# Another order for the first layer's step: low part of g on VectorE, gathered decode, Tanh first

## The chip, the cores and the metric

One core of one Trainium2 chip runs the whole program. The metric is the device time of one execution in microseconds (us); the kernel before took 1130.29 us in the median of 3 runs (1128.52 to 1130.34).

## The reference

Three stages, each feeding the next, on 1792 tokens of width 768 (4 batches of 448, 12 heads of 64):

```python
scores = (q @ k.T) / sqrt(64) - log(448)
x = (1 / (1 + exp(-scores))) @ v           # sigmoid attention, no softmax
h = x @ w_in                               # first layer, 768 -> 2048
x = (h - tanh(h)) @ w_out                  # 2048 -> 768
gate = 1 / (1 + exp(-(x @ w_gate)))        # second layer, 768 -> 1536
out = (gate * (x @ w_val)) @ w_out2        # 1536 -> 768
```

The weights arrive as 64-bit words that the kernel turns into float32 itself. Where h is small, h - tanh(h) cancels, so the kernel replaces it there by a polynomial in h.

## The kernel before, in words

Every operand of a product is held as two parts: a rounded high part and a low part, the value minus its high part. A product is three matmuls (high x high, high x low, low x high; `mm3`, L363 to 368, whose matmuls all have L365).

The attention stage runs first. The first layer then runs as 32 steps, i = 0 to 31: the hidden features are cut into 8 pairs of 128-blocks, and each pair is run for the 4 batches in turn (i // 4 is the pair, i % 4 the batch). In iteration i of the loop (L899 to L939) TensorE computes the hidden product of step i+1 (`hidden_mm`, tile ph, 36 matmuls) and then the output product of step i in six groups of six matmuls, one per block of 128 output columns (`project_group`, tiles po, index 0 to 5). Beside it, ScalarE, VectorE and GpSimd turn ph of step i+1 into g, which is the operand of the next iteration's output product.

The order on each engine is written out by hand: it is the order in which the program issues the instructions, and each engine runs its own in that order. What the functions issue:

- `hidden_act` (L385) gives ScalarE's `sq` (u = Square of ph, L399), `th` (y = Tanh, L402), `cut` (mask mk from u, L405), `q1` and `q2` (two inner squares s from the mask, L408, L411), and VectorE's `a` (y = h - Tanh, L414), `b` (L417, needs u), `c` (L422, needs the first inner square), `d` (L427, needs the second) and `e`: the mask copy COPY_PREDICATED (L432, writes y where the mask holds), after which ScalarE makes the high part of g (L433). `f` is the low part of g (L437), two GpSimd instructions of half the columns; it is issued one iteration later, as `rest` (L907).
- `step` (L502) places all of this among the six groups. Groups 1, 3 and 5 are evicted into the accumulator by ScalarE (`post`, L523), and before that their bank is filled with the old accumulator by ScalarE (a seed: `seed`, L454, `pre` in `step`); groups 0, 2 and 4 are evicted with an add by VectorE (L472). Seeds exist in steps 4 to 28; from step 29 on all groups are evicted by VectorE. The po tiles share four PSUM banks, and a new tile takes the bank that the program let go first.
- `decode1` (L182) turns one first-layer weight into its two parts, one weight per iteration: Abs on ScalarE (L145), four VectorE instructions (L148, L151, L157, L163), the fetch of a later weight by SP (L135), and then the split: a copy on ScalarE (L175) and two low parts on GpSimd (L178). There is one tile m for all of them. The pieces stand at fixed places: Abs in `ex[2]`, the VectorE pieces at the head of the next iteration (`todo`), the split in `ex[0]`.
- `keeping` (L196) decodes a weight of the second layer ahead of time in four pieces: Abs on ScalarE; the two mask steps (L148, L151); the first merge (L157); the second merge (L163) with the next fetch and the store to DRAM on SP (kept, L215). There is one tile mk for it, so the next Abs must wait for the store. `some` (L895) issues these pieces, two at the head of an iteration, the third in `ex[1]`, the fourth in `ex[2]`; three iterations of four do one weight (and all from 24 to 26).
- From iteration 27 on (`tail`) the places `ex` also hold work for the second layer: the load and split of its first weights, the operands (L592, L594) and sums (L578).

Of the kernel before, what the change touches and what calls it, by code (L numbers as in the profile page):

```python
# [8 lines left out]
F32 = mybir.dt.float32  # L9
# [3 lines left out]
ALU = mybir.AluOpType  # L13
# [19 lines left out]
def kernel(  # L33
# [12 lines left out]
    nc = tc.nc  # L46
# [135 lines left out]
    def decode1(u):  # L182
        m = dp.tile([128, WC], I32, tag="m", name=f"m{u}", padded_shape=[128, 2 * WC])

        def d():
            n, w = w_alloc(f"w{u}", [128, 2, KD, 128])
            rounded(w, m.bitcast(F32), f"w{u}")
            w_t[u] = n, w

        a, b, c, c2 = decode(u, m)  # L190
        return [a, b, lambda: (c(), c2()), d]

    kept = {}
    early = []
# [175 lines left out]
    def hidden_mm(i):  # L370
        g, t = divmod(i, NB)
        ph = psa.tile([128, 2, 512], F32, tag="pa", name=f"ph{i}")
        for j in range(2):
            n, w = w_t[4 * g + j]
            for c in range(KD):
                xt = x[t][c // KH]
                mm3(
                    ph[:, j, :S], lambda a: w[:, a, c], lambda a: xt[:, a, c % KH],
                    c == 0, c == KD - 1,
                )  # L380
            if t == NB - 1:
                w_free.append(n)
        h_t[i] = ph

    def hidden_act(i):  # L385
        ph = h_t.pop(i)
        h = ph[:, :, :S]
        gt = gp.tile([128, 2, 2, S], F32R, tag="g", name=f"g{i}")
        if i == 0:
            gp.tile([128, GGAP], F32, tag="ggap", name="ggap", bufs=1)  # L390
        g_t[i] = gt
        uu = tp.tile([128, 2, S], F32, tag="u", name=f"u{i}")
        y = tp.tile([128, 2, S], F32, tag="y", name=f"y{i}")
        mk = tp.tile([128, 2, S], F32, tag="mk", name=f"mk{i}")
        s1 = tp.tile([128, 2, S], F32, tag="s1", name=f"s1{i}")
        s2 = tp.tile([128, 2, S], F32, tag="s2", name=f"s2{i}")

        def sq():
            nc.scalar.activation(out=uu, in_=h, func=AF.Square)  # L399

        def th():
            nc.scalar.activation(out=y, in_=h, func=AF.Tanh)  # L402

        def cut():
            nc.scalar.activation(out=mk, in_=uu, func=AF.Relu, bias=gb[:, 2:3], scale=-1.0)  # L405

        def q1():
            nc.scalar.activation(out=s1, in_=mk, func=AF.Square, bias=gb[:, 0:1], scale=-1.0)  # L408

        def q2():  # L410
            nc.scalar.activation(out=s2, in_=mk, func=AF.Square, bias=gb[:, 1:2], scale=-1.0)  # L411

        def a():
            nc.vector.tensor_tensor(out=y, in0=h, in1=y, op=ALU.subtract)  # L414

        def b():
            nc.vector.scalar_tensor_tensor(  # L417
                out=h, in0=uu, scalar=G_C, in1=h, op0=ALU.mult, op1=ALU.mult
            )

        def c():
            nc.vector.scalar_tensor_tensor(  # L422
                out=h, in0=s1, scalar=G_B1, in1=h, op0=ALU.add, op1=ALU.mult
            )

        def d():
            nc.vector.scalar_tensor_tensor(  # L427
                out=h, in0=s2, scalar=G_B2, in1=h, op0=ALU.add, op1=ALU.mult
            )

        def e():
            nc.vector.copy_predicated(y, mk.bitcast(I32), h)  # L432
            nc.scalar.activation(out=gt[:, 0], in_=y, func=AF.Copy)  # L433

        def f():
            for j in range(2):
                nc.gpsimd.tensor_tensor(  # L437
                    out=gt[:, 1, j], in0=y[:, j], in1=gt[:, 0, j].bitcast(F32), op=ALU.subtract
                )

        return [sq, th, cut, q1, q2], [a, b, c, d, e, f]

# [9 lines left out]
    def seed(name, at, d):  # L452
        po = pb_tile(name)
        nc.scalar.activation(out=po[:, :S], in_=at[:, d], func=AF.Copy)  # L454
        return po

    def project_group(name, at, gt, outs, d, first, dst=None, po=None, evict=True):

        seeded = po is not None
        if not seeded:  # L460
            po = pb_tile(name)
        for j, (_, w) in enumerate(outs):
            mm3(
                po[:, :S], lambda a: w[:, a, d], lambda a: gt[:, a, j],
                j == 0 and not seeded, j == len(outs) - 1, seeded,
            )
        if not evict:
            return po
        if first:
            nc.vector.tensor_copy(out=at[:, d], in_=po[:, :S])  # L470
        else:
            nc.vector.tensor_tensor(out=at[:, d], in0=po[:, :S], in1=at[:, d], op=ALU.add)  # L472
        if dst is not None:
            nc.sync.dma_start(out=dst, in_=at[:, d])
# [4 lines left out]
    def outs1(i):  # L479
        g, t = divmod(i, NB)  # L480
        if g == 0:
            acc[t] = acc_tile(t, f"acc{i}")
        return acc[t], g_t.pop(i), [w_t[4 * g + 2], w_t[4 * g + 3]]
# [13 lines left out]
    def run(fs):  # L497
        for f in fs:
            f()
        fs.clear()  # L500

    def step(i, act, dve, extra, po):  # L502

        g, t = divmod(i, NB)
        at, gt, outs = outs1(i)
        sq, th, cut, q1, q2 = act
        a, b, c, d_, e = dve

        def pre(d):
            if g and i < LASTSEED:  # L510
                po[d] = seed(f"po{i}_{d}", at, d)

        def group(d):
            by_act = d % 2 == 1 and i < LASTSEED
            p = project_group(
                f"po{i}_{d}", at, gt, outs, d, g == 0, None, po.get(d), not by_act
            )
            po[d] = p

        def post(d):  # L520
            if i >= LASTSEED:
                return
            nc.scalar.activation(out=at[:, d], in_=po[d][:, :S], func=AF.Copy)  # L523

        ex = extra + [None] * 6
        sq()
        th()
        group(0)
        a()
        pre(3)  # L530
        cut()
        group(1)
        b()
        run(ex[0] or [])
        group(2)
        q1()
        post(1)
        c()
        run(ex[1] or [])
        pre(5)  # L540
        q2()
        group(3)
        d_()
        run(ex[2] or [])
        post(3)
        group(4)
        e()
        run(ex[3] or [])
        group(5)
        post(5)  # L550
        run(ex[4] or [])
        if t == NB - 1:
            w_free.extend(n for n, _ in outs)

# [268 lines left out]
    with tc.manual_schedule():  # L823
# [19 lines left out]
        todo = []  # L843
        nxt = [0]
        for p in range(NP):
# [3 lines left out]
            if p >= 3 and not todo and nxt[0] < NEARLY:  # L849
                todo = decode1(nxt[0])  # L850
# [36 lines left out]
        todo = []  # L887
# [4 lines left out]
            early += keeping(j)  # L892
        TAIL = N1 - 5

        def some(kind):  # L895
            if early and len(early) % 4 == kind and (i < TAIL or kind) and (i % 4 or i > TAIL - 4):
                early.pop(0)()

        for i in range(N1 - 1):  # L899
            hidden_mm(i + 1)  # L900
            po = {}
            if NB <= i < LASTSEED:
                po[1] = seed(f"po{i}_1", acc[i % NB], 1)
            if todo:
                todo.pop(0)()
            if rest:
                rest.pop()()  # L907
            if todo:
                todo.pop(0)()
            some(0)  # L910
            some(3)
            act, dve = hidden_act(i + 1)
            ex = [[], [], [], [], []]
            if todo:
                ex[0].append(todo.pop(0))
                nxt[0] += 1
            if nxt[0] < wanted(i + 1):
                todo = decode1(nxt[0])
                ex[2].append(todo.pop(0))
            ex[1].append(lambda: some(2))  # L920
            ex[2].append(lambda: some(1))
            rest = [dve.pop()]
            tail = i - TAIL
            if tail == 0:
                ex[3].append(lambda: load_m(0))
            elif tail == 1:
                for at in range(4):
                    ex[at].append(first_split.pop(0))
            elif tail == 2:
                ex[0].append(lambda: operand(0, "a11", nc.vector))  # L930
                ex[1].append(first_split.pop(0))
                ex[2].append(first_split.pop(0))
            elif tail == 3:
                operand(0, "s1", nc.gpsimd)
                operand(0, "s2", nc.gpsimd)
                ex[2].append(lambda: operand(0, "a12", nc.gpsimd))
                ex[3].append(lambda: sums("s4"))
                ex[4].append(lambda: sums("s3"))
            step(i, act, dve, ex, po)  # L939
        rest.pop()()  # L940
        tp_ctx.close()
# [99 lines left out]
```

## Time and profile before

| what | value |
|---|---|
| median of 3 runs | 1130.29 us (1128.52 to 1130.34) |
| the profiled execution's own time | 1127.33 us |
| its span, first to last instruction | 1125.4 us |
| granted TensorE clock, mean | 0.998 |
| busy TensorE / VectorE / ScalarE / GpSimd | 1091.5 / 806.8 / 608.8 / 522.7 us |

The profile is one execution. A busy share is an average over all stages, so this document reads the first layer's loop (about 153 to 628 us) alone. In the rows, PE is TensorE's matmul, PEld its weight load, DVE VectorE, ACT ScalarE, POOL GpSimd, SP the engine that issues DMAs; "out<-in" gives the tiles, L the line; in brackets stands how long the engine was idle before and whose end released it.

### The profile page before, as it was taken

The numbers are of one execution on the slowest core, as the hardware profiler recorded it, in microseconds if no ns is written. First come the engines' busy times: TensorE is split into PE (matmuls) and PEld (weight loads), VectorE is DVE, ScalarE is ACT, GpSimd is POOL, SyncE is SP. The second block draws the span as 40 slices with busy tenths as digits, with TensorE's granted clock in tenths as the row PEclk, the third lists the DMA queues.
The fourth block names the chain that finished last, engine by engine and source line by source line (L and its number), as shares of the span: only waits on it lengthen the run. The fifth ranks groups of instructions, "written<-read, shape, count | busy, mean of one in ns | idle before, by whom it ended". The sixth has DMA issues, their size and how long they took to land.

```text
span 1125.4 us, 15990 instructions
## 1 busy us (share of the span) xinstructions
PE 1091.5 (97%) x6085; PEld 967.6 (86%) x6085; DVE 806.8 (72%) x1083; ACT 608.8 (54%) x855; POOL 522.7 (46%) x475
## 2 busy tenths in 40 slices
PE   9999989999999999999999989999998999999998
PEld 5677779888989898988898888998997899999997
DVE  4778646888898888889867988988468545354444
ACT  6778645666667676667666444444336234334320
POOL 5455301433433343443336657675466755446540
PEclk9999999999999999999999999999999999999999
DMA  7766301424232324233320156464112411111202
GB/s 197 188 187 190 112 1 43 141 98 129 87 124 90 121 99 140 98 118 121 116 68 29 59 172 218 149 209 163 55 46 69 142 70 56 57 56 62 80 1 98
DMA packets 40204, 119.79 MB, mean 106 GB/s; under 512 B 6080, under 2 KB 21440, under 8 KB 40128
## 3 DMA queue, kind: packets, MB, share of 16 engines
q1 hardware_dynamic: 36896, 116.38, 31.8%
q0 software_dynamic: 3072, 2.17, 0.9%
q8 instruction: 48, 0.79, 0.3%
q10 hardware_dynamic: 160, 0.23, 0.1%
q14 instruction: 28, 0.23, 0.1%
HBM read 99.09 MB, written 19.66 MB: 106 GB/s over the span
## 4 chain that ended last, share of the span: by engine, by line
PE 60%; DVE 14%; ACT 9%; DMA 9%; issue 5%; POOL 3%; SPq 1%; ACTq 0%; DVEq 0%; POOLq 0%
PE pq L365 14%; PE ph L365 10%; DMA kept<-mk 8%; PE pb L365 6%; PE po L365 6%; PE pa L365 6%; PE pc L365 5%; PE pv L349 5%; PE sa L314 4%; PE pe L365 3%; DVE ph L422 2%; DVE ph L427 2%; ACT mk L405 1%; ACT y L402 1%; PE sl L326 1%
## 5 line engine op out<-in xcount | busy, mean ns | idle before, releaser
L365 PE MATMUL po<-g,w 128*128 128x448 f32 x1152 | 247.7, 367 | 10.3 <-DVE acc L472 6.0
L365 PEld LDWEIGHTS po<-g,w 128*128 128x128 f32 x1152 | 211.7, 188 | 40.5 <-POOL g L437 11.6
L365 PE MATMUL ph<-x,w 128*128 128x448 f32 x1152 | 235.8, 362 | 0.2 <-ACT at L318 0.2
L365 PEld LDWEIGHTS ph<-x,w 128*128 128x128 f32 x1152 | 215.8, 187 | 15.3 <-ACT at L318 0.6
L437 POOL TENSOR_TENSOR g<-y,g 128x448 fp32r<-128x448 f32 x64 | 114.0, 1801 | 194.8 <-issue 166.1
L365 PE MATMUL pq<-gg,w 128*128 128x448 f32 x864 | 183.8, 363 | 5.1 <-POOL gg L742 2.4
L365 PEld LDWEIGHTS pq<-gg,w 128*128 128x128 f32 x864 | 161.4, 187 | 18.7 <-POOL gg L742 3.1
L178 POOL TENSOR_TENSOR w_t<-mm,w_t 128x384 fp32r<-128x384 f32 x92 | 101.1, 1128 | 119.7 <-ACT w_t L175 54.1
L178 POOL TENSOR_TENSOR w<-m,w 128x384 fp32r<-128x384 f32 x64 | 63.6, 1017 | 113.2 <-ACT w L175 80.9
L472 DVE TENSOR_TENSOR acco<-pq,acco 128x448 f32<-128x448 f32 x120 | 72.2, 619 | 33.4 <-PE pq L365 32.9
L365 PE MATMUL pa<-a,w_b 128*128 128x448 f32 x432 | 94.2, 362 | 0.0
L365 PEld LDWEIGHTS pa<-a,w_b 128*128 128x128 f32 x432 | 81.0, 187 | 5.4
L472 DVE TENSOR_TENSOR acc<-po,acc 128x448 f32<-128x448 f32 x93 | 57.3, 618 | 26.6 <-PE po L365 26.6
L433 ACT ACTIVATE g<-y 128x896 fp32r<-128x896 f32 x32 | 30.6, 956 | 81.3 <-DVE y L432 81.3
L318 ACT ACTIVATE at<-sa,bias_s 128x896 f32<-128x896 f32 x72 | 67.3, 1008 | 8.0 <-PE sa L314 7.9
L178 POOL TENSOR_TENSOR w<-mm,w 128x384 fp32r<-128x384 f32 x44 | 48.5, 1124 | 45.5 <-ACT w L175 43.3
L742 POOL TENSOR_TENSOR gg<-sg,gg 128x448 fp32r<-128x448 f32 x44 | 62.5, 1451 | 12.3 <-ACT gg L739 12.3
L175 ACT ACTIVATE w_t<-mm 128x768 fp32r<-128x768 f32 x48 | 40.0, 842 | 48.5 <-DVE mm L646 34.8
L175 ACT ACTIVATE w_b<-mm 128x768 fp32r<-128x768 f32 (+1 forms) x48 | 32.5, 680 | 62.2 <-PE pb L365 30.0
L178 POOL TENSOR_TENSOR w_b<-mm,w_b 128x384 fp32r<-128x384 f32 x46 | 51.3, 1138 | 23.1 <-ACT w_b L175 12.1
L349 PE MATMUL pv<-at,vt 128*64 128x224 f32 x576 | 61.0, 362 | 0.0
L349 PEld LDWEIGHTS pv<-at,vt 128*64 128x64 f32 x576 | 39.9, 139 | 19.8 <-issue 8.3
(102 smaller groups left out, 1880.2 us busy)
## 6 DMA issues: line engine op xcount, KB each, us to landing
mm<-kept SPq DMA_DIRECT2D x36, 768.0 KB, 4.2
st<-in_w_out_dram SPq DMA_DIRECT2D x28, 768.0 KB, 4.5
st<-in_w_in_dram SPq DMA_DIRECT2D x16, 768.0 KB, 4.3
st<-in_w_gate_dram SPq DMA_DIRECT2D x12, 768.0 KB, 4.9
st<-in_w_val_dram SPq DMA_DIRECT2D x12, 768.0 KB, 5.0
kept<-mk SPq DMA_DIRECT2D x21, 384.0 KB, 5.6
kept<-mq SPq DMA_DIRECT2D x15, 384.0 KB, 5.5
kt<-in_k_dram SPq DMA_DIRECT2D x48, 112.0 KB, 4.0
```

The costliest lines, as they stand in the source:

```text
L175: nc.scalar.activation(out=w0, in_=mf, func=AF.Copy)
L178: (low or nc.gpsimd).tensor_tensor(out=w1[:, r], in0=mf[:, r], in1=w0[:, r].bitcast(F32), op=ALU.subtract)
L314: nc.tensor.matmul(pa[:, j, :S], kk[r, ki, c], qq[r, qi], start=(i == 0), stop=(i == 2),)
L318: nc.scalar.activation(out=at[:, :, c], in_=pa[:, :, :S], func=AF.Sigmoid, bias=bias_s, scale=qk_scale,)
L349: nc.tensor.matmul(po[j * D:(j + 1) * D, h, :SH], vt[:, j, c], at[:, j, c, h * SH:(h + 1) * SH], start=False, stop=(c == NCH - 2),)
L365: nc.tensor.matmul(o, w(i), xv(j), start=first and n == 0, stop=last and n == 2, skip_group_check=seeded,)
L422: nc.vector.scalar_tensor_tensor(out=h, in0=s1, scalar=G_B1, in1=h, op0=ALU.add, op1=ALU.mult)
L427: nc.vector.scalar_tensor_tensor(out=h, in0=s2, scalar=G_B2, in1=h, op0=ALU.add, op1=ALU.mult)
L433: nc.scalar.activation(out=gt[:, 0], in_=y, func=AF.Copy)
L437: nc.gpsimd.tensor_tensor(out=gt[:, 1, j], in0=y[:, j], in1=gt[:, 0, j].bitcast(F32), op=ALU.subtract)
L472: nc.vector.tensor_tensor(out=at[:, d], in0=po[:, :S], in1=at[:, d], op=ALU.add)
L742: low.tensor_tensor(out=gt[t][:, 1, j], in0=sg[t][:, j], in1=gt[t][:, 0, j].bitcast(F32), op=ALU.subtract,)
```

## The change

The low part of g becomes one VectorE instruction over all 896 columns instead of two GpSimd instructions. In the step, Tanh goes ahead of Square; the mask and then the seed of group 3 follow; `b` and the first inner square come ahead of group 1; the eviction `post(1)` and the second inner square come ahead of group 2; and the split of the decoded weight (`ex[0]` before, `ex[1]` now) stands behind the second inner square and the seed of group 5. `some` goes: the four pieces of a second-layer weight are issued together at the head of the iteration, behind the low part of g and the first-layer decode, which follow the mask copy on VectorE. The number of weights decoded so early stays the same.

```diff
         def f():
-            for j in range(2):
-                nc.gpsimd.tensor_tensor(
-                    out=gt[:, 1, j], in0=y[:, j], in1=gt[:, 0, j].bitcast(F32), op=ALU.subtract
-                )
+            nc.vector.tensor_tensor(
+                out=gt[:, 1], in0=y, in1=gt[:, 0].bitcast(F32), op=ALU.subtract
+            )
...
-        ex = extra + [None] * 6
+        th()
         sq()
-        th()
         group(0)
         a()
+        cut()
         pre(3)
-        cut()
+        b()
+        q1()
         group(1)
-        b()
-        run(ex[0] or [])
-        group(2)
-        q1()
+        run(extra[0])
         post(1)
         c()
-        run(ex[1] or [])
+        q2()
+        group(2)
         pre(5)
-        q2()
+        run(extra[1])
         group(3)
         d_()
-        run(ex[2] or [])
+        run(extra[2])
         post(3)
...
-        def some(kind):
-            if early and len(early) % 4 == kind and (i < TAIL or kind) and (i % 4 or i > TAIL - 4):
-                early.pop(0)()
-
...
-            some(0)
-            some(3)
+            if early and i < TAIL and (i % 4 or i > TAIL - 4):
+                run(early[:4])
+                del early[:4]
             act, dve = hidden_act(i + 1)
             ex = [[], [], [], [], []]
             if todo:
-                ex[0].append(todo.pop(0))
+                ex[1].append(todo.pop(0))
                 nxt[0] += 1
...
-            ex[1].append(lambda: some(2))
-            ex[2].append(lambda: some(1))
             rest = [dve.pop()]
```

## Rows read from the trace of the kernel before

**Rows 1.** Busy us in one decode step: length, PE, PEld, DVE, ACT, POOL, clock, DMA, GB/s

```profile
376.13:391.70 15.57, 15.02 (x74) 13.27 (x73) 13.44 (x17) 10.45 (x16) 5.74 (x4) 1.00 0.41 127
```

**Rows 2.** Timeline of TensorE: start us, length us, engine, line, operation, tiles, count [idle, releaser]

```profile
167.24 7.36 PE L365 MATMUL ph<-x,w 128*128 128x448 f32 x36
...
475.10 7.39 PE L365 MATMUL po<-g,w 128*128 128x448 f32 x36
...
489.52 5.28 PE L365 MATMUL po<-g,w 128*128 128x448 f32 x24
495.25 2.75 PE L365 MATMUL po<-g,w 128*128 128x448 f32 x12 [0.45 <-DVE acc L472]
...
603.71 7.36 PE L365 MATMUL ph<-x,w 128*128 128x448 f32 x36
```

**Rows 3.** Who waited for whom over the whole span: us in total, times, longest

```profile
ACT mk L145 <- DMA kept<-mk: 40.8, 15, 3.9
...
ACT m L145 <- POOL w L178: 3.3, 6, 0.6
```

**Rows 4.** Timeline of all engines in a decode step that lost time

```profile
490.03 0.90 ACT L145 ACTIVATE mk<-st 128x768 f32<-128x768 f32 x1 [2.58 <-DMA kept<-mk]
...
494.58 0.62 DVE L472 TENSOR_TENSOR acc<-po,acc 128x448 f32<-128x448 f32 x1
```

**Rows 5.** Timeline, a VectorE merge beside GpSimd's low part of g

```profile
409.60 3.75 POOL L437 TENSOR_TENSOR g<-y,g 128x448 fp32r<-128x448 f32 x2 [4.58 <-issue]
...
410.53 1.80 DVE L163 SCALAR_TENSOR_TENSOR m<-st,m 128x768 int32<-128x768 int32 x1
```

**Rows 6.** Groups of instructions by shape, whole span: count, busy us, mean ns

```profile
L178 POOL TENSOR_TENSOR w<-m,w 128x384 fp32r<-128x384 f32 x64 | 63.6, 1017 | 113.2 <-ACT w L175 80.9 <-PE po L365 32.2
...
L163 DVE SCALAR_TENSOR_TENSOR mk<-st,mk 128x768 int32<-128x768 int32 x21 | 20.0, 952 | 0.0
...
L178 DVE TENSOR_TENSOR w_t<-mm,w_t 128x768 fp32r<-128x768 f32 x2 | 1.9, 954 | 0.0
```

**Rows 7.** Timeline of ScalarE in an undisturbed step, T = 475.10

```profile
475.30 0.92 ACT L399 ACTIVATE u<-ph 128x896 f32<-128x896 f32 x1 [2.69 <-PE ph L365]
476.11 0.91 ACT L402 ACTIVATE y<-ph 128x896 f32<-128x896 f32 x1
...
476.91 0.56 ACT L454 ACTIVATE po<-acc 128x448 f32<-128x448 f32 x1
...
477.37 1.05 ACT L405 ACTIVATE mk<-u,gb 128x896 f32<-128x896 f32 x1
...
478.31 0.84 ACT L175 ACTIVATE w<-m 128x768 fp32r<-128x768 f32 x1
479.04 1.04 ACT L408 ACTIVATE s<-mk,gb 128x896 f32<-128x896 f32 x1
...
479.98 0.54 ACT L523 ACTIVATE acc<-po 128x448 f32<-128x448 f32 x1
...
480.40 0.55 ACT L454 ACTIVATE po<-acc 128x448 f32<-128x448 f32 x1
```

**Rows 8.** Timeline, two ScalarE neighbours of which the second needs the first

```profile
614.80 1.04 ACT L405 ACTIVATE mk<-u,gb 128x896 f32<-128x896 f32 x1
...
615.87 1.04 ACT L408 ACTIVATE s<-mk,gb 128x896 f32<-128x896 f32 x1
```

**Rows 9.** Timeline of step 28, where the seed of group 5 came late

```profile
581.67 6.17 PE L365 MATMUL po<-g,w 128*128 128x448 f32 x30
...
587.38 0.56 ACT L454 ACTIVATE po<-acc 128x448 f32<-128x448 f32 x1
...
589.31 7.36 PE L365 MATMUL ph<-x,w 128*128 128x448 f32 x36
```

**Rows 10.** The page's DMA issues: count, KB each, us to landing

```profile
kept<-mk SPq DMA_DIRECT2D x21, 384.0 KB, 5.6
```

**Rows 11.** Timeline, TensorE at the tail's first wait for GpSimd

```profile
612.99 6.68 PE L365 MATMUL po<-g,w 128*128 128x448 f32 x32 [1.12 <-POOL g L437]
```

More of the change, by code (lines that the diff above doesn't have):

```diff
@@ L547, in step @@
         e()
-        run(ex[3] or [])
+        run(extra[3])
         group(5)
         post(5)
-        run(ex[4] or [])
+        run(extra[4])
         if t == NB - 1:
```

## The prediction

> **What bounds the kernel now.** I first asked for the busy times by stretch: in a first-layer step of 15.57 us that also decodes a weight for the second layer, TensorE is busy 15.02 us, VectorE 13.44, ScalarE 10.45, GpSimd 5.74, at granted clock 1.00 [rows 1]. TensorE is the bound, so the change can be worth only what a step takes beyond its matmuls. How long these take is in the order of TensorE's work: an undisturbed step (hidden product, then six groups of six matmuls) takes 603.71 - 589.31 = 14.40 us [rows 2, 9]; from the second hidden product (167.24) to the last (603.71) 29 steps take 436.47 us where 29 x 14.40 = 417.6 would do [rows 2]. **18.9 us are lost**, 0.65 a step, and this is all that the loop can give back.
>
> What causes the loss: ScalarE waits for the store of the decoded weight, 40.8 us in 15 waits [rows 3]. Abs of the next weight (L145) overwrites the tile being stored; it starts at 490.03, 2.58 us late [rows 4], and Square and Tanh of the step stand behind it on ScalarE. VectorE's second add (L472), behind a and b, which need them, runs 494.58 to 495.20 [rows 4], and the fifth group (index 4) starts at 495.25, 0.45 idle [rows 2], as it needs that add: its bank is that of group 2. 13 decode steps show this wait and lose some 1.1 us each; the rest goes in smaller waits.
>
> **The change, part by part.** Times are counted from T, the start of a step's first output group (475.10 in [rows 2], where Square starts at T+0.20 [rows 7]).
>
> (1) Low part of g. GpSimd loses two instructions a step. VectorE gains one, whose shape isn't in the trace: the 128x768 subtraction took 0.954 us [rows 6], by columns x 896/768 = 1.1 us; the ends are 0.95 and 1.8 (the length when GpSimd is in its way). VectorE also gets something back: with GpSimd's low part running, the last merge L163 of a decode took 1.80 us [rows 5], without it 0.952 [rows 6], so 0.85. Net VectorE has 13.44 + 1.1 - 0.85 = 13.7 us in a decode step, under 14.40.
>
> (2) Gathered decode. All four pieces and the DMA issues (next fetch, store) now follow the mask copy, the other decode and the low part, instead of the merges standing between later steps. No instruction is added; SP issues the two DMAs earlier in the step, behind the fetch for the other decode. A store took 5.5 to 5.6 us to land [rows 10]; issued about T+17.3 (2.6 into the next step) it lands at about T+8 there, and Abs needs the tile at T+12 (below). The waits of 40.8 us in sum go, and with them the late second add.
>
> (3) ScalarE's new order, each start from spacings of rows. Tanh T+0.20; Square 0.81 later (475.30 to 476.11) = 1.01. The mask now follows Square directly and needs it: dependent neighbours start one duration and 0.03 apart (614.80, 1.04 long, to 615.87 [rows 8]), so 0.91 + 0.03 = 0.94: 1.95; bounds 0.81 (plain spacing) and 1.07. Seed of group 3: 0.94 on (mask-like instruction to its successor, 479.04 to 479.98) = 2.89, ends 3.44. First inner square: 0.46 on (476.91 to 477.37) = 3.35. Eviction post(1): 0.94 on = 4.29, ends 4.84. Second square: 0.42 on (479.98 to 480.40) = 4.71. **Seed of group 5**: 0.94 on = 5.65, ends 6.20 [rows 7]. In the kernel before it ended at 480.95, T+5.85.
> What TensorE does with a late seed: at 581.67 + 6.00 = 587.67 group 5 was due, its seed (587.38, 0.56 long) ended 587.94, and the next hidden product came at 589.31, 7.64 - 7.20 = 0.44 late [rows 9]: a group starts 0.17 after its seed ends. So group 5 starts at 6.20 + 0.17 = 6.37 where 6.00 was due: **0.36 us lost in each step**. Group 3 (3.44 + 0.17 = 3.61, due 3.60) loses nothing. Banks are handed out in the order in which the program lets them go; as post(1) now stands ahead of group 2, group 4 gets group 1's bank: 4.84 + 0.17 = 5.01, due 4.80, 0.2 late, inside the 0.36 (not added). With the 0.13 either way of the unseen Square-to-mask step the price is 0.2 to 0.5.
> Seeds exist in steps 4 to 28. Steps 4 to 27: 24 x 0.36 = 8.6. In step 28 the first piece of the next layer's split (a ScalarE copy, 0.74 on the queue) stands ahead of post(1), so group 5 starts 1.1 late. Loop loss after: 8.6 + 1.1 = 9.7.
>
> (4) Weight split behind the second square. Copy at about T+6.1 to 6.9, two GpSimd parts of 1.017 each [rows 6] to T+9.0. There is one tile m: the next Abs waits for GpSimd (it did so at times before, 3.3 us in 6 waits [rows 3]). Behind that wait on ScalarE are post(3), the copy g (T+10.3), post(5), the next step's seed 1 (ends T+12.2) and Abs of the gathered weight (T+12 to 13). Tanh is wanted at T+14.96 (a step of 14.76, and 0.20), so 2 us of cover; without it each us late would be a us of TensorE. VectorE waits too: its decode starts at T+10.0; then the low part ends at about 12.3, and TensorE wants it at 14.9. Two decodes of at most 0.95 per instruction (8) and 1.1 are 8.7 us, so VectorE reaches the next first add at the latest 3.9 after the next T; the seed of group 5, at 5.65, is the first to want that add. Cost: nothing; the cover is the 1.7 us between 3.9 and 5.65.
>
> (5) Tail. Group 0 of step 30 waited 1.12 for GpSimd [rows 11]; this goes, but VectorE, which sets the tail (sums, operands), takes two low parts of 1.1 and an operand split behind a later square. Ends: gain 1.1, loss 1.5; I take a gain of 0.5, as the sums run without GpSimd beside them.
>
> **Sum.** 18.9 - 9.7 + 0.5 = 9.6 us. The profiled execution took 1127.33 (span 1125.4), so 1117.7; the median of the runs stands 3.0 above it, 1130.29: **1120.7**.
>
> **Rivals.**
> A: the seed is in time after all (ScalarE's neighbours overlap more than their rows say): only step 28 loses, gain 18.9 - 1.1 + 0.5 = 18.3, 1112.0. For: seed 5 was only 0.35 earlier before, and cost TensorE nearly nothing. Against: [rows 9] price exactly such a lateness. 0.23.
> B: VectorE becomes the bound. Place: its queue between Abs of m (T+10) and the mask copy. With no 0.85 back, and the low part at 1.8, a decode step needs 13.44 + 1.8 = 15.2 and waits of some 0.2 for the copy g: 15.4; the 18 such steps among 4 to 27 lose up to 1.0 each, the six between them 0.36, step 28 1.1: at most 21.3, and less by what VectorE catches up in the six, so about the 18.9 of now: 1130, no change. Against: once GpSimd is done with the split, nothing of it runs beside VectorE's decode. 0.11. The Trainium skill's page Perfetto Trace Analysis (Optimizing Scalar/DVE Operations) speaks this way: with a saturated VectorE, work may move off it, even to GpSimd, though the two share a port so it might not help; the change goes the other way with VectorE at 86%. By that rule the time would be this rival's; the trace bears out its second half: 1.80 against 0.952.
> C, slower: group 4 keeps group 2's bank, so that it waits for the second add, which now stands behind c, and c behind the first inner square (T+4.4). The add then ends at about T+6.6, group 4 starts at 6.8 where 4.8 was due: 2.0 a step, 24 x 2.0 + 1.1 = 49 lost instead of 18.9: about 1160. It decides as soon as that add ends after T+4.6. For: the wait is there before [rows 2]. Against: the order of release, above. 0.06.
> That the gathered block doesn't free Abs (the store still lands late) would leave 1128 to 1130: 0.04.
>
> **How the numbers follow.** Forecast 0.56, with 0.2 to 0.5 a step 1117 to 1124.5 and the tail's ends 1116 to 1126. The range reaches to A, and up to part of B: 1110.5 to 1128; outside are C and most of B. A measurement of this kernel can tell about 0.2% (2.3 us) from no change. Faster: the forecast, A and a part of the rest, 0.84; same: half of B and of the last, 0.07; slower 0.09.
>
> **What would show it.** Hidden products 14.4 apart in steps 1 to 3 and 14.7 to 14.8 from step 4 on; TensorE's waits in the loop named ScalarE's L454, 0.3 to 0.4 each, none by L472 or GpSimd; no wait of Abs for the store, but one of about 2 us for GpSimd's split; L163 at 0.95. I am wrong if steps are 14.40 (A), if VectorE is busy without gaps and steps are 15 or more (B), or if group 4 waits for L472 (C).

## The result and the profile after

The changed kernel takes 1119.26 us in the median of 4 runs (1116.63 to 1120.31), the kernel before, run beside it, 1129.4 (1127.36 to 1130.34). The ratio is 0.9909, 95% interval 0.9885 to 0.9933: 10 us faster, between 7.6 and 13. The forecast was 1120.7. The profiled execution took 1120.31 us (span 1118.5), the slowest of the four.

The busy times of one step of the loop with a second-layer decode (length, then PE, PEld, DVE, ACT, POOL, granted clock, DMA share, GB/s), the answer to [rows 1]:

```profile
357.99:372.75 14.76, 14.76 (x73) 13.28 (x72) 13.79 (x18) 10.60 (x15) 1.99 (x3) 1.00 0.42 128
```

The step is 14.76 us instead of 15.57. VectorE has 13.79 us where it had 13.44, GpSimd 1.99 where it had 5.74. TensorE's matmul records now leave no gap (busy 14.76 of 14.76), so what a step loses shows only in the distance between the starts of the hidden products (TensorE's timeline, the answer to [rows 2]):

```profile
167.12 7.36 PE L365 MATMUL ph<-x,w 128*128 128x448 f32 x36
...
181.52 7.36 PE L365 MATMUL ph<-x,w 128*128 128x448 f32 x36
...
357.99 7.36 PE L365 MATMUL ph<-x,w 128*128 128x448 f32 x36
365.19 7.73 PE L365 MATMUL po<-g,w 128*128 128x448 f32 x36
372.75 7.36 PE L365 MATMUL ph<-x,w 128*128 128x448 f32 x36
...
577.53 2.84 PE L365 MATMUL po<-g,w 128*128 128x448 f32 x12 [0.65 <-ACT acc L522]
580.20 7.36 PE L365 MATMUL ph<-x,w 128*128 128x448 f32 x36
...
594.60 7.36 PE L365 MATMUL ph<-x,w 128*128 128x448 f32 x36
```

From the second hidden product to the last, 427.48 us pass where there were 436.47: **9.0 us came from the loop**. The steps without seeds take 14.40 (167.12 to 181.52), every step with seeds 14.76 or 14.77 (357.99 to 372.75), and step 28 takes 15.49 (564.71 to 580.20), with the wait of 0.65 at 577.53 in it. What TensorE's weight loads wait for in steps 4 to 28 (us in total, times, longest):

```profile
PEld po L365 <- ACT acc L522: 7.8, 25, 1.0
PEld po L365 <- ACT po L453: 6.5, 25, 0.3
```

Two waits in each of 25 steps, both for ScalarE: the eviction post(1) (now L522) ahead of group 4 and the seed (now L453) ahead of group 5. The waits for VectorE's second add and for GpSimd's low part of g are gone, and so is the wait of Abs for the store. What has grown is the wait of Abs for GpSimd's split, 3.3 us in 6 waits before [rows 3], and behind it stands one of VectorE (whole span):

```profile
ACT m L145 <- POOL w L178: 55.1, 30, 2.2
...
DVE m L148 <- ACT m L145: 17.8, 24, 1.3
```

The new instruction L436 and the merge L163 that shared its time with GpSimd before (groups by shape; compare [rows 5, 6]):

```profile
L436 DVE TENSOR_TENSOR g<-y,g 128x896 fp32r<-128x896 f32 x32 | 35.0, 1092 | 7.5 <-ACT g L433 4.6
...
L163 DVE SCALAR_TENSOR_TENSOR m<-st,m 128x768 int32<-128x768 int32 x32 | 30.7, 958 | 1.1
```

ScalarE's queue in a step with T = 365.19, to be laid beside [rows 7]:

```profile
365.38 0.92 ACT L402 ACTIVATE y<-ph 128x896 f32<-128x896 f32 x1 [1.97 <-PE ph L365]
...
366.20 0.91 ACT L399 ACTIVATE u<-ph 128x896 f32<-128x896 f32 x1
...
367.14 1.05 ACT L405 ACTIVATE mk<-u,gb 128x896 f32<-128x896 f32 x1
...
368.10 0.53 ACT L453 ACTIVATE po<-acc 128x448 f32<-128x448 f32 x1
...
368.56 1.03 ACT L408 ACTIVATE s<-mk,gb 128x896 f32<-128x896 f32 x1
...
369.50 0.52 ACT L522 ACTIVATE acc<-po 128x448 f32<-128x448 f32 x1
369.92 1.03 ACT L411 ACTIVATE s<-mk,gb 128x896 f32<-128x896 f32 x1
...
370.86 0.53 ACT L453 ACTIVATE po<-acc 128x448 f32<-128x448 f32 x1
```

The seed of group 5 ends at 371.39, T+6.20. Square to mask is 0.94, as between dependent neighbours in [rows 8].

### The profile page after: what moved, and what is told of

Its sections match the earlier page's. It is cut to its first block, busy times and chain, and to the rows that moved or that the text cites. A ratio compares the mean times of both kernels' runs of the same rounds, so it can differ in the third digit from the quotient of the medians.

```text
span 1118.5 us, 15946 instructions
## 1 busy us (share of the span) xinstructions
PE 1091.0 (98%) x6085; PEld 967.8 (87%) x6085; DVE 816.3 (73%) x1115; ACT 613.2 (55%) x855; POOL 407.9 (36%) x411
## 4 chain that ended last, share of the span: by engine, by line
PE 87%; DVE 5%; ACT 3%; POOL 2%; issue 1%; DMA 1%; SPq 0%; ACTq 0%; DVEq 0%
PE ph L365 21%; PE po L365 20%; PE pq L365 14%; PE pb L365 6%; PE pa L365 6%; PE pc L365 6%; PE pv L349 5%; PE sa L314 4%; PE pe L365 3%; PE sl L326 1%; POOL a L592 1%; PE pv L342 1%; POOL gg L740 1%; DVE mq L157 0%; DMA st<-in_w_in_dram 0%
## 5 line engine op out<-in xcount | busy, mean ns | idle before, releaser
L471 DVE TENSOR_TENSOR acco<-pq,acco 128x448 f32<-128x448 f32 x120 | 72.2, 619 | 33.4 <-PE pq L365 32.9
L402 ACT ACTIVATE y<-ph 128x896 f32<-128x896 f32 x32 | 29.4, 920 | 78.4 <-PE ph L365 78.4
L471 DVE TENSOR_TENSOR acc<-po,acc 128x448 f32<-128x448 f32 x93 | 57.1, 618 | 20.3 <-PE po L365 20.3
L145 ACT ACTIVATE m<-st 128x768 f32<-128x768 f32 x32 | 28.9, 903 | 56.7 <-POOL w L178 55.1
```

The source lines that it names most:

```text
L145: nc.scalar.activation(out=mf, in_=hi.bitcast(F32), func=AF.Abs)
```

## The experiments

Each run is a change of one of the two kernels, timed beside the kernel before; ratios are to the kernel before, with their 95% intervals, and a comparison with the changed kernel is by the medians. Beside these runs the kernel before had medians of 1128.4 to 1128.7, and 1129.4 beside the changed kernel, so a comparison with the changed kernel by medians carries up to 1 us from that alone.

### The second inner square behind the seed

```diff
         c()
-        q2()
         group(2)
         pre(5)
+        q2()
```

> The changed kernel with one instruction moved: the second inner square goes behind the seed of group 5. My theory: what is left of the loop's loss, 0.37 us a step (14.77 instead of 14.40), is the late seed of group 5 (0.36), under which the late eviction post(1) for group 4 (0.2) is hidden. Then the seed ends about T+5.3 and only post(1) is left: hidden products 14.60 apart in steps 4 to 27, 24 x 0.17 = 4 us faster than the changed kernel, and the one wait of TensorE's weight load that remains in the loop is for L522. If the bound were VectorE or the wait of Abs for GpSimd's split (2.16 us in each step), the distance stays 14.77 and the time stays the same. If the seed alone were the cause, 14.40 and 9 us.

1115.11 us, ratio 0.9878 (0.986 to 0.9896), 4 us under the changed kernel. TensorE's hidden products:

```profile
356.54 7.36 PE L365 MATMUL ph<-x,w 128*128 128x448 f32 x36
...
371.15 7.36 PE L365 MATMUL ph<-x,w 128*128 128x448 f32 x36
```

14.60 and 14.61 in all steps from 4 to 27; the only wait of the weight loads left in the loop is for L522, 25 times. So the seed was the last thing that a step waited for, with the eviction hidden under it, and both terms have the size that was worked out: 0.36 and 0.20.

### The split back in its old place

```diff
-                ex[1].append(todo.pop(0))
+                ex[0].append(todo.pop(0))
```

> The changed kernel with the split of the decoded weight back ahead of the eviction post(1) and the second inner square. My theory: its ScalarE copy takes 0.73 of the queue, so the eviction, the second square and the seed of group 5 come 0.73 later and each step takes 14.77 + 0.73 = 15.50, as step 28 does in the changed kernel: 24 x 0.73 = 17.5 us slower than the changed kernel, 7 slower than the kernel before. If the place of the split is free (because what it delays is hidden), the distance stays at 14.77; if VectorE were the bound, the earlier release of Abs would make it faster by up to 2 us a step.

1135.86 us, ratio 1.007 (1.0055 to 1.0085): 16.6 us slower than the changed kernel. Steps of 15.50:

```profile
380.52 7.36 PE L365 MATMUL ph<-x,w 128*128 128x448 f32 x36
...
396.02 7.36 PE L365 MATMUL ph<-x,w 128*128 128x448 f32 x36
```

One ScalarE copy ahead of the eviction is worth 0.73 us a step (15.50 - 14.77). Without moving the split the whole change loses 7 us against the kernel before.

### The second-layer decode spread again

```diff
-            if early and i < TAIL and (i % 4 or i > TAIL - 4):
-                run(early[:4])
-                del early[:4]
+            some(0)
+            some(3)
...
+            ex[1].append(lambda: some(2))
+            ex[2].append(lambda: some(1))
```

> The changed kernel with the second-layer decode spread over the step again (Abs and the two mask steps at the head, the merges in the places of the kernel before, so the store leaves some 9 us after T instead of 2.6 after the next). My prediction said that gathering takes the waits for the store away and with them 1.1 us in 13 steps: then the waits of L145 for the store come back and the kernel is about 13 us slower than the changed one. A rival: the new order on ScalarE does most of it, because the gathered weight's Abs now stands behind the wait for GpSimd's split, about T+12, and the store lands at T+14.4, so ScalarE waits some 2 us where it had nothing else to do: the wait is back in the rows, but Tanh of the next step is only about 0.3 late in 18 steps, 5 us slower or less.

1131.37 us, ratio 1.0022 (1.0008 to 1.0036): 12.1 us slower than the changed kernel. The rival that I had come to doubt the prediction by was wrong; the prediction's step stands. ScalarE and SP around one store:

```profile
377.29 0.43 SPq L215 DMA_DIRECT2D kept<-mk  x1
...
382.87 0.89 ACT L145 ACTIVATE mk<-st 128x768 f32<-128x768 f32 x1 [2.05 <-DMA kept<-mk]
...
383.67 0.90 ACT L402 ACTIVATE y<-ph 128x896 f32<-128x896 f32 x1
```

The store leaves at 377.29, and Abs of the next weight, held until 382.87, pushes Tanh to 383.67, about 0.8 behind the end of the hidden product, in the 13 steps behind a store: 15.5 to 15.8 there, once 16.25, and 14.77 elsewhere. I had expected the store some 9 us after T. It leaves at T+9.4 in the step before (361.65, T = 352.28), and at T+10.25 in the one shown (T = 367.04), whose ScalarE work is already 0.9 late from the step before it (its Tanh starts at 368.13, T+1.09 instead of T+0.20). The merge L163 and GpSimd's split also stand side by side in this run, and take 1.1 and 2.7 us there instead of 0.96 and 2.0.

### The low part of g back on GpSimd

```diff
-            nc.vector.tensor_tensor(
-                out=gt[:, 1], in0=y, in1=gt[:, 0].bitcast(F32), op=ALU.subtract
-            )
+            for j in range(2):
+                nc.gpsimd.tensor_tensor(
+                    out=gt[:, 1, j], in0=y[:, j], in1=gt[:, 0, j].bitcast(F32), op=ALU.subtract
+                )
```

> The changed kernel with the low part of g back on GpSimd in two instructions. My theory: the loop's 14.77 is set on ScalarE's queue, so the place of the low part is nearly free there: L163 of the first decode takes 1.8 us again, VectorE has one instruction less, the low part ends about T+15.0, just when the next Tanh wants to write the tile that it reads, so 0 to 0.1 a step; in the tail the two waits for GpSimd come back. In all 0 to 5 us slower. If moving the low part is what made the gain, the kernel goes back to the time of the one before, 10 us slower; if VectorE is the bound of the changed kernel, it is faster by up to 1 us a step.

1121.53 us, ratio 0.9938 (0.9923 to 0.9952): 2.3 us slower than the changed kernel by the medians, though the two ranges of runs overlap. The profile is clearer: steps take 14.85, 0.08 more (one takes 15.12), because Tanh waits until GpSimd has read the tile that Tanh overwrites (over the span):

```profile
ACT y L402 <- POOL g L437: 52.9, 23, 3.2
```

In this order the engine of the low part matters little in the loop, and what it costs there is this wait. Group 4 waits for no add of VectorE in this run either, so the low part on VectorE isn't what frees it.

### Only the low part on VectorE, all else as before

The edit is the first hunk of the change alone, on the kernel before.

> The kernel before with the low part of g on VectorE and nothing else changed. My theory: the 13 waits behind the store stay (1.1 us each), the waits of the output groups for GpSimd (five of 0.3, two of about 0.5, two in the tail) go, and L163 of the first decode falls from 1.80 to 0.95, which pays for the 1.1 of the new instruction. 2 to 3 us faster in the loop, the tail within 1: 1 to 4 us faster than the kernel before. If VectorE is the bound (my prediction's rival B), 5 to 15 us slower.

1123.74 us, ratio 0.9961 (0.9947 to 0.9974): 4.6 us faster than the kernel before, a little more than expected. The rows of the profile hold less of it: the loop gave 1.7 (601.10 - 166.34 = 434.76, before 436.47) and the tail 0.9; where the rest comes from was not found. The waits for GpSimd are gone and 13 steps still take 15.4 to 15.8 (one 16.6), because the wait for the store is all there (steps 1 to 28):

```profile
ACT mk L145 <- DMA kept<-mk: 41.5, 15, 3.7
```

VectorE is not the bound with the new instruction, in the old order either.

### Only the gathered decode, all else as before

The edit is the last part of the change alone (the diff of the spread run, backwards), on the kernel before.

> The kernel before with the four pieces of the second-layer decode gathered at the head of the iteration and nothing else changed. If the wait for the store is the whole cause of the loss, it goes, and the kernel is about 13 us faster, steps near 14.5. My theory: the wait goes from the rows, but group 4 still takes group 2's bank in the old order and so needs VectorE's second add; the gathered block and the first decode, which both meet GpSimd's low part, hold VectorE until about T+2.5 to 3, the second add ends near T+5.6 where group 4 wants it at 4.6, and decode steps take about 15.4: within 4 us of the kernel before.

1125.03 us, ratio 0.9967 (0.9951 to 0.9982): 3.4 us faster. Abs waits for no store, and the steps come in fours of 14.43, 15.86, 14.78 and 15.5. VectorE and TensorE in one of them, T = 384.30:

```profile
386.87 0.62 DVE L472 TENSOR_TENSOR acc<-po,acc 128x448 f32<-128x448 f32 x1
...
389.40 0.61 DVE L472 TENSOR_TENSOR acc<-po,acc 128x448 f32<-128x448 f32 x1
...
390.07 2.68 PE L365 MATMUL po<-g,w 128*128 128x448 f32 x12 [0.80 <-DVE acc L472]
```

VectorE comes out of the gathered block and reaches its first add at 386.87, T+2.6, its second add ends at 390.01, and group 4 starts at 390.07, 0.80 idle (18 such waits, 18.3 us in the weight loads). So the wait for the store was only the first of two in a row: without it the same group waits for the same add, now for the decode itself. In the changed kernel group 4 needs no add any more: the rows name L522 there. The old order with both the low part and the gathered decode was not run, nor the new order by itself.

### ScalarE's order written anew

```diff
         a()
-        cut()
         pre(3)
+        cut()
         b()
-        q1()
         group(1)
-        run(extra[0])
         post(1)
-        c()
-        q2()
         group(2)
         pre(5)
+        q1()
+        c()
+        q2()
+        run(extra[0])
         run(extra[1])
```

> The changed kernel with ScalarE's order of a step written anew: Tanh, Square, seed of group 3, mask, eviction post(1), seed of group 5, and only then the two inner squares and the split; groups 1 and 2 with VectorE's second add ahead of c. My theory: post(1) ends about T+3.8 and the seed of group 5 about T+4.2 (limits 4.63 and 5.83), VectorE reaches its first add at T+2.8 and has 14.0 us of work and waits in a decode step, so nothing is left to wait for: hidden products 14.40 apart in all steps to 28, 24 x 0.37 + 1.1 = 10 us faster than the changed kernel, about 20 faster than the kernel before. If VectorE or the split on GpSimd is the next bound, 14.6 to 14.8 and 0 to 5 us.

1109.35 us, ratio 0.984 (0.9817 to 0.9863): **10 us faster than the changed kernel and 19 faster than the one before**, and the best of the versions. Every step takes 14.40, the time of its 72 matmuls:

```profile
367.96 7.36 PE L365 MATMUL ph<-x,w 128*128 128x448 f32 x36
...
382.36 7.36 PE L365 MATMUL ph<-x,w 128*128 128x448 f32 x36
```

TensorE's weight loads wait for nothing in the loop. Abs waits for GpSimd's split as long as ever (steps 1 to 28), and VectorE is as busy:

```profile
ACT m L145 <- POOL w L178: 51.9, 24, 2.2
```

So neither of these cost TensorE anything in the changed kernel; the 9.9 us that its loop still lost were the seeds and the eviction behind the squares and, in step 28, behind a copy of the split.

### In addition, group 1 right behind group 0

```diff
         group(0)
+        group(1)
         a()
...
         b()
-        group(1)
         post(1)
```

> As the run before, and group 1 is issued right behind group 0, ahead of a, so that in the last steps, where VectorE evicts every group, its add for group 1 no longer stands behind a and b. My theory: the loop is the same (14.40); group 5 of step 30, which waited 2.04 us for that add in the changed kernel, starts on time; the group 0 that follows still waits for the sums and the low part. 1 to 2 us faster than the run before. If the sums set the end of the tail, the same time as the run before, with a longer wait later.

1111.54 us, ratio 0.9857 (0.9833 to 0.988); the loop is the same, the run no faster than the one above, by its median 2.2 us slower, with intervals that overlap. TensorE after the last hidden product:

```profile
585.88 7.37 PE L365 MATMUL ph<-x,w 128*128 128x448 f32 x36
...
601.14 1.97 PE L365 MATMUL pa<-a,w_b 128*128 128x448 f32 x9
...
608.28 3.48 PE L365 MATMUL pb<-s,w_t 128*128 128x448 f32 x9 [3.36 <-ACT pb L720]
```

The second layer's first product comes 15.26 us after the last hidden product (601.14 - 585.88) instead of 16.93, as expected, and the third product (pb) then waits 3.36 instead of 1.04, for a copy that ScalarE makes behind the high part of g, which waits for the mask copy on VectorE. So by these rows the tail hangs on VectorE's chain, and starting one group earlier only moved the wait. The product behind it also took 3.48 instead of 2.08 us, which is the clock of this one execution (last section).

### Square ahead of Tanh again

```diff
-        th()
         sq()
+        th()
```

> The changed kernel with Square ahead of Tanh again, nothing else. My theory: VectorE's a waits for the second of the two in either order (in the changed kernel's tail it starts 0.03 after Square ends, with Tanh long done), so Tanh in front wins nothing; but with Tanh in between, the mask no longer follows Square directly and starts 0.81 behind its neighbour instead of 0.94, so that every later start on ScalarE is 0.13 earlier: hidden products 14.64 apart instead of 14.77, 24 x 0.13 = 3 us faster than the changed kernel. If Tanh ahead of Square lets a start earlier, and that matters, the steps stay at 14.77 and the tail gets longer by up to 1 us.

1114.95 us, ratio 0.9884 (0.9867 to 0.99): 4.3 us faster than the changed kernel. ScalarE in a step with T = 363.09:

```profile
363.29 0.92 ACT L399 ACTIVATE u<-ph 128x896 f32<-128x896 f32 x1 [1.96 <-PE ph L365]
364.11 0.92 ACT L402 ACTIVATE y<-ph 128x896 f32<-128x896 f32 x1
364.90 1.04 ACT L405 ACTIVATE mk<-u,gb 128x896 f32<-128x896 f32 x1
...
368.60 0.55 ACT L453 ACTIVATE po<-acc 128x448 f32<-128x448 f32 x1
```

Square to mask is now 1.61 with Tanh between, not 0.81 + 0.94 = 1.75, and the seed of group 5 ends at T+6.06. Steps take 14.62. Tanh ahead of Square, one piece of the change's third part, thus costs 0.15 us a step. It does not shorten the tail either, where a starts right behind the second of the two in both orders.

## Why the prediction was right

**The bound and the loss.** TensorE stayed the bound; of the 18.9 us that the loop took over its matmuls, 9.9 remain (29 steps: 427.48 - 417.6), where 9.7 were forecast. The run with ScalarE's order written anew takes the rest away, so that the loss was all in waits, as said.

**(1) Low part of g.** 1.092 us (forecast 1.1), and L163 of the first decode went from 1.80 to 0.958, so that VectorE has 13.79 us in a decode step where 13.7 were forecast. Put back on GpSimd it costs 2.3 us by the medians, by itself it brings 4.6.

**(2) Gathered decode.** The waits for the store went, and the kernel without this part is 12 us slower. The prediction's account of the loss was short in one place: it named the store as what made the second add late. The run with the gather alone shows a second cause behind it, VectorE's own decode work, which keeps the wait for that add alive in the old order. The forecast was not hurt, since it took the new bank order into the sum.

**(3) ScalarE's order.** 0.36 us a step, from spacings of rows and the price of one late seed: 0.36 to 0.37 measured, and the seed ends at T+6.20 as worked out. The hidden 0.20 of group 4 came out when the seed was moved; the list of signs had left it out, and named only the seed's wait. Step 28 lost 1.09 (forecast 1.1).

**(4) The split.** Abs waits about 2 us for GpSimd in each step, as forecast (2.16 in the step read above), and VectorE starts its decode at T+10.05, 0.57 late; with both still there, steps of 14.40 are possible, so the cover held.

**(5) The tail**, the term that was wrong, though small: a gain of 0.5 was taken, and from the last hidden product to the second layer's first product it lost 0.9 us (611.33 - 594.60 = 16.73, before 619.50 - 603.71 = 15.79). The first wait for GpSimd did go [rows 11]; in its place group 5 of step 30 waits 2.04 for the add of group 1 (L471 at 609.34), which is behind a and b. The end of the stretch in the kernel before, and the timeline of all engines in the changed one:

```profile
619.50 1.96 PE L365 MATMUL pa<-a,w_b 128*128 128x448 f32 x9
```

```profile
592.73 1.70 DVE L592 TENSOR_TENSOR a<-acc,a 128x448 fp32r<-128x448 f32 x3 [0.75 <-ACT a L590]
...
605.59 0.90 ACT L402 ACTIVATE y<-ph 128x896 f32<-128x896 f32 x1
606.39 0.91 ACT L399 ACTIVATE u<-ph 128x896 f32<-128x896 f32 x1
607.34 1.09 DVE L414 TENSOR_TENSOR y<-ph,y 128x896 f32<-128x896 f32 x1 [2.48 <-ACT u L399]
...
609.34 0.62 DVE L471 TENSOR_TENSOR acc<-po,acc 128x448 f32<-128x448 f32 x1
...
610.01 1.48 PE L365 MATMUL po<-g,w 128*128 128x448 f32 x6 [2.04 <-DVE acc L471]
...
611.33 1.96 PE L365 MATMUL pa<-a,w_b 128*128 128x448 f32 x9
```

The two low parts on VectorE, which the term counted as a cost, are not what lost the time. In the run with the low part alone the same stretch takes 14.86, 0.9 less than before:

```profile
601.10 7.36 PE L365 MATMUL ph<-x,w 128*128 128x448 f32 x36
...
615.96 1.96 PE L365 MATMUL pa<-a,w_b 128*128 128x448 f32 x9
```

The loss comes with the new order, in two pieces that make 1.85 of the 1.87 us between that run and the changed kernel. In step 29 VectorE is idle 0.75 for ScalarE's copy of the first operand (the row at 592.73), which now stands behind the first inner square, and the mask copy starts 3.34 after the last hidden product instead of 2.49 (597.94 - 594.60, 603.59 - 601.10). In step 30 b (608.34) stands ahead of the add of group 1 (609.34), 1.0 us, where the order before had it behind. The prediction counted the first among its losses, as an operand split behind a later square, and left out the second. a starts 0.04 after Square ends (607.30), not after Tanh, so that Tanh in front wins nothing here. The bounds given for this term, a gain of 1.1 and a loss of 1.5, hold the value.

**The rivals.** A (no price of the seed) falls by the two waits in 25 steps and the steps of 14.77; B (VectorE the bound) falls by the steps of 14.40 with the same VectorE work: at 13.79 of 14.76 us it was busy, and not the bound. The Trainium skill's page Perfetto Trace Analysis (Optimizing Scalar/DVE Operations) says that moving work off VectorE may make sense if it is saturated. That condition was not met here: work was moved onto VectorE, and the 1.092 us a step cost the loop nothing that shows. C (group 4 bound to the second add) falls by the release of group 4, which is L522. That the store still lands late falls too, as Abs waits for no store.

**The sum.** Forecast 9.6 us (9.7 with the terms as printed, which are rounded), measured 10 by the medians. The rows hold less: the loop gave 9.0 and the tail took 0.9, which makes 8.1. The profiled executions stand only 7.0 apart (1127.33 and 1120.31), and most of what is left, some 1.2 us, went in the second layer, which the change does not touch, where the clock fell once, as told below. The profiled execution is thus 2.6 over its forecast of 1117.7, and the median 1.4 under its own, since the 3.0 added for the distance from profile to median came out as 1.05 the other way. That the two totals agree so closely is in part luck; the interval, 7.6 to 13, holds 8.1 as well as 10. What bears the mechanism out are the steps and their waits.

## What to carry to other kernels

When a wait is taken away, look for the next thing that is late at the same place: here the store, VectorE's decode and ScalarE's queue stood one behind the other. The gathered decode alone brought 3.4 us, and the rest of the change without it nothing (1131.37 us). On an in-order queue every instruction ahead of the one that the bound engine waits for costs its spacing, step after step (0.73 us for one copy here), so work that feeds only the next step (the squares, the split) goes behind the seeds and evictions that feed this one. A price for such an order can be had from the spacings of neighbours in the old trace, if dependent and independent neighbours are kept apart.

## What the runs showed that I had not expected

TensorE's clock can fall after a wait in one execution and not in another. In the profiled execution of the changed kernel a product that waited 2.07 us for VectorE took 3.59 us for its nine matmuls; the stretch around it (columns as above) and the product:

```profile
645.00:650.00 5.00, 3.10 (x8) 2.80 (x9) 4.90 (x7) 0.04 (x1) 3.12 (x3) 0.68 0.25 84
```

```profile
646.90 3.59 PE L365 MATMUL pc<-a,w_t 128*128 128x448 f32 x9 [2.07 <-DVE pe L759]
```

The granted clock of these 5 us is 0.68, a mean over its two levels (1.2 and 2.4 GHz). The same product took 2.08 us after a wait of 2.18 in the kernel before and after one of 2.06 in the run with ScalarE's order written anew. Of two more runs, the one with Square ahead of Tanh shows 3.59 there after a wait of 2.05, and the one with the second inner square behind the seed 2.08 after 2.08. A comparison of two single executions would have put these 1.5 us down to the change. In the run with group 1 right behind group 0 another product, after 3.36 us of waiting, lost 1.4 us (3.48 for nine). What decides whether the clock falls was not tried.
